# Butterflies on VectorE ahead of half-size TensorE steps, and S tiles split by DMA

## The chip, the cores and the metric

The kernel runs on one core of a Trainium2 chip. The metric is device time in microseconds. TensorE multiplies matrices from SBUF into PSUM, VectorE and ScalarE work on elements, GpSimd (POOL) is nearly unused before, SyncE (SP) issues DMAs in the order of its instructions. All DMAs run on 16 shared DMA engines. Every engine executes its own instructions strictly in program order.

## The reference

Two independent blocks, their results side by side in the last dimension:

```python
# A: Fourier mixing, real part; x is 2048 x 512
a = jnp.einsum("bsd,ed->bse", x, dft_hid_re)
b = jnp.einsum("bsd,ed->bse", x, dft_hid_im)
y = jnp.einsum("ts,bse->bte", dft_seq_re, a) - jnp.einsum("ts,bse->bte", dft_seq_im, b)
# B: a long convolution per channel (512 channels, length 2048, 128 states)
P = jnp.exp((A * dt[:, None])[:, :, None] * pos[None, None, :])
K = 2.0 * jnp.einsum("dn,dnl->dl", C, P).real
Kf = jnp.fft.rfft(K, L2)          # L2 = 4096
Uf = jnp.fft.rfft(u_t, L2)
y = jnp.fft.irfft(Uf * Kf[None, :, :], L2)[:, :, :L]
y = y + u * D_skip
```

Everything is float32. Inputs are random, but the DFT matrices of A are given as inputs.

## The kernel before

**Block A (class `Fnet`)** swaps the two products: it first multiplies S, the 2048 x 2048 sequence matrices (real and imaginary), with x, and then the result P with the small matrices W. Each product is made of three matmuls in the fast format `F32R`: an operand is split into `hi` (rounded to F32R) and `lo` (the rest), and hi·hi, hi·lo and lo·hi are summed in PSUM (L327, tile `acc`). x and W stay in SBUF; S and P stream by in tiles of 128 x 512. There are 8 groups of S (4 column blocks t, real and imaginary c) with 16 tiles each, 128 in all, and then 4 groups of P with 8 tiles each. A tile is used by 4 x 3 matmuls. Each finished group is copied out of PSUM by ScalarE (L350) and stored: S groups to the DRAM tiles `p` (L355), P groups to the output (L358).

A streamed tile goes through `load`: SP issues the DMA into `raw` (L295; 4 buffers, `RAWS`), ScalarE makes `hi` by a copy with rounding (L207), VectorE makes `lo = raw - hi` (L211). There are 3 pairs of hi and lo (`DEPTH`), given back when TensorE has used them. P tiles are read back from DRAM by the same path.

**Block B (class `Ssm`)** makes the kernel K from tables of powers of the state factors: VectorE builds tables by products and sums (`mul` L566, `add` L575) for 16 chunks of 32 channels, and TensorE sums over the states (`taps`, L762). Then it does the long convolution as an FFT in two steps, with fp32 matmuls on parts of the array (`tile_position`):

- first step on u, `stage1_u` (L835), 8 groups of two l2 pairs; result through ScalarE (L845) to DRAM `xu`;
- first step on K, `stage1_k` (L792), 8 groups of 64 channels; ScalarE (L801) into `xk_sb`, stored to DRAM `xk`. GpSimd adds the D skip to the first tap ahead of it (L785);
- second step on both, `product` (L913), for 4 quarters h of the channels and 4 parts q of the frequencies; ScalarE copies (L926), VectorE multiplies the two spectra (L929 to L942);
- first step of the inverse in the same function (L949), written through ScalarE (L964) to DRAM `zs`. While taps are left, its matmuls run right behind a `taps` group (`Joined`);
- last step of the inverse, `inverse` (L995), 2 groups per quarter h; ScalarE (L1001), output store (L1004).

The order of all this is made when the program is built: `Plan` simulates every engine with prices (`act`, `dve`, `load`, and numbers in the `yield` lines), and always emits next what it thinks can start first, with an urgency. What comes out is one fixed order for each engine and for SP's queue. A generator that yields a `Sem` waits there for a buffer; `banks` hands out two pairs of PSUM banks to all of block B, and `give` returns one. Block A's matmuls have a low urgency and fill TensorE whenever nothing of block B is ready.

## Time and profile before

| | |
|---|---|
| three runs | 594.92, 598.23, 600.19 us; median 598.23 |
| profiled execution, span from the first to the last instruction | 595.6 us |
| TensorE busy | 585.1 us (98%) |
| VectorE busy | 495.7 us (83%) |
| ScalarE busy | 381.0 us (64%) |
| GpSimd busy | 5.3 us (1%) |
| DMA | 125.97 MB, mean 212 GB/s |

The profile gives no time of the profiled execution other than its span; the launch and what lies after the last instruction are not in it. Busy times are sums over instructions, and matmuls overlap in the pipeline, so a busy TensorE is not yet one at its peak. A group of the table names line, engine, operation, what is written and read, the shape and the count; then its busy time, the mean duration in ns, and the idle time of the engine just before with what ended it. In the chain of work that ended last, every piece is a start, a duration, and an engine with its line.

### The profile page before, as it was taken

The numbers are of one execution on the slowest core, as the hardware profiler recorded it, in microseconds if no ns is written. First come the engines' busy times: TensorE is split into PE (matmuls) and PEld (weight loads), VectorE is DVE, ScalarE is ACT, GpSimd is POOL, SyncE is SP. The second block draws the span as 40 slices with busy tenths as digits, with TensorE's granted clock in tenths as the row PEclk, the third lists the DMA queues.
The fourth block names the chain that finished last, engine by engine and source line by source line (L and its number), as shares of the span: only waits on it lengthen the run. The fifth ranks groups of instructions, "written<-read, shape, count | busy, mean of one in ns | idle before, by whom it ended". The sixth has DMA issues, their size and how long they took to land.

```text
span 595.6 us, 16944 instructions
## 1 busy us (share of the span) xinstructions
PE 585.1 (98%) x6982; PEld 451.6 (76%) x6982; DVE 495.7 (83%) x883; ACT 381.0 (64%) x745; POOL 5.3 (1%) x12
## 2 busy tenths in 40 slices
PE   8999999999999999999899999999989999999997
PEld 6767668788788777777687787778767887777775
DVE  6977989999999999999699999999979973253620
ACT  5789884947586596758374976677655625354522
POOL 0000000000000000000000000000000000000000
PEclk9999999999999999999999999999989999999999
DMA  8999995363593376454778593478668745899674
GB/s 264 321 360 344 333 339 186 107 177 94 128 279 100 102 193 216 141 148 122 237 213 245 149 279 120 132 213 257 207 202 253 249 126 168 223 348 276 204 256 149
DMA packets 141246, 125.97 MB, mean 212 GB/s; under 512 B 46192, under 2 KB 106352, under 8 KB 140912
## 3 DMA queue, kind: packets, MB, share of 16 engines
q1 hardware_dynamic: 140880, 124.48, 68.2%
q8 instruction: 55, 0.90, 0.6%
q10 hardware_dynamic: 288, 0.39, 0.3%
q14 instruction: 23, 0.19, 0.1%
HBM read 82.12 MB, written 42.73 MB: 210 GB/s over the span
## 4 chain that ended last, share of the span: by engine, by line
PE 79%; DVE 12%; DMA 3%; issue 3%; ACT 2%; SPq 0%; DVEq 0%; ACTq 0%
PE acc L327 61%; PE f L913 4%; PE f L762 4%; DVE prod L566 4%; PE f L995 3%; DVE lo L211 3%; PE f L835 3%; DVE t L575 3%; PE f L949 2%; PE f L792 2%; DMA raw<-in_sT 1%; DMA xt_u<-xu 1%; DVE z L929 1%; DMA p<-y 1%; DMA xt_k<-xk 1%
## 5 line engine op out<-in xcount | busy, mean ns | idle before, releaser
L327 PE MATMUL acc<-hi,x_hi 128*128 128x512 f32 x640 | 257.7, 403 | 3.7 <-ACT y L350 1.9
L327 PE MATMUL acc<-lo,x_hi 128*128 128x512 f32 x640 | 250.7, 392 | 0.1
L327 PE MATMUL acc<-hi,x_lo 128*128 128x512 f32 x640 | 250.0, 391 | 0.1
L566 DVE TENSOR_TENSOR prod<-t,cs 128x1024 f32<-128x1024 f32 (+4 forms) x192 | 164.1, 871 | 7.5 <-ACT t L704 5.6
L327 PEld LDWEIGHTS acc<-hi,x_hi 128*128 128x128 f32 x640 | 120.2, 188 | 49.6 <-issue 20.1
L211 DVE TENSOR_TENSOR lo<-raw,hi 128x512 fp32r<-128x512 f32 x160 | 109.4, 687 | 53.8 <-ACT hi L207 48.9
L207 ACT ACTIVATE hi<-raw 128x512 fp32r<-128x512 f32 x160 | 100.3, 628 | 76.9 <-PE acc L327 56.8
L327 PEld LDWEIGHTS acc<-hi,x_lo 128*128 128x128 f32 x640 | 120.5, 188 | 26.7 <-issue 0.6
L327 PEld LDWEIGHTS acc<-lo,x_hi 128*128 128x128 f32 x640 | 120.5, 188 | 24.3 <-DVE lo L211 1.4
L575 DVE TENSOR_TENSOR t<-prod 128x512 f32<-128x512 f32 (+4 forms) x192 | 94.3, 513 | 1.2
L582 ACT ACTIVATE square<-t 128x256 f32<-128x256 f32 (+1 forms) x64 | 36.5, 571 | 25.3 <-DVE t L575 23.2
L350 ACT ACTIVATE y<-acc 128x512 f32<-128x512 f32 x47 | 27.7, 595 | 17.3 <-PE acc L327 9.8
L926 ACT ACTIVATE uk<-f 128x1024 f32<-128x1024 f32 x32 | 31.6, 1015 | 6.4 <-PE f L913 6.4
L762 PEld LDWEIGHTS f<-t,t 128*32 128x32 f32 x2048 | 29.4, 110 | 6.5 <-issue 5.0
L762 PE MATMUL f<-t,t 128*32 128x64 f32 x2048 | 32.2, 220 | 0.3 <-issue 0.3
L929 DVE TENSOR_TENSOR z<-uk 128x512 f32<-128x512 f32 x32 | 22.0, 687 | 12.4 <-ACT uk L926 10.1
L641 ACT ACTIVATE cs<-cs 128x352 f32<-128x352 f32 x32 | 15.9, 536 | 17.9 <-DVE cs L636 17.9
L964 ACT ACTIVATE z<-f 128x512 f32<-128x512 f32 x32 | 17.7, 594 | 11.4 <-PE f L762 7.4
L595 DVE TENSOR_TENSOR t<-square 128x128 f32<-128x128 f32 (+1 forms) x64 | 24.8, 387 | 0.0
L913 PE MATMUL f<-xt_k,w 64*32 64x128 f32 x1024 | 23.1, 271 | 0.5 <-issue 0.5
L589 DVE SCALAR_TENSOR_TENSOR t<-t 128x128 f32<-128x128 f32 (+2 forms) x48 | 22.4, 467 | 0.3
L931 DVE TENSOR_TENSOR uk<-uk 128x512 f32<-128x512 f32 x32 | 22.1, 689 | 0.7
(85 smaller groups left out, 444.8 us busy)
## 6 DMA issues: line engine op xcount, KB each, us to landing
raw<-in_sT SPq DMA_DIRECT2D x127, 256.0 KB, 3.7
p<-y SPq DMA_DIRECT2D x32, 256.0 KB, 4.1
xt_u<-xu SPq DMA_DIRECT2D x32, 256.0 KB, 4.4
xk<-xk_sb SPq DMA_DIRECT2D x32, 256.0 KB, 4.0
xt_k<-xk SPq DMA_DIRECT2D x32, 256.0 KB, 5.5
zs<-z SPq DMA_DIRECT2D x32, 256.0 KB, 3.4
zl<-zs SPq DMA_DIRECT2D x16, 512.0 KB, 6.1
raw<-p SPq DMA_DIRECT2D x32, 256.0 KB, 4.2
```

The costliest lines, as they stand in the source:

```text
L207: self.nc.scalar.activation(hi, src, AF.Copy)
L211: self.nc.vector.tensor_tensor(lo, src, hi.bitcast(F32), op=OP.subtract)
L327: nc.tensor.matmul(acc[d], l[:, cols], r, start=k == 0 and n == 0, stop=k == len(items) - 1 and n == 2)
L350: self.nc.scalar.activation(y, ps, AF.Copy, scale=-1.0 if g[2] == 1 else 1.0)
L566: self.nc.vector.tensor_tensor(p.rearrange("p k d c m -> p k (d c) m"), src.rearrange("p d c l -> p (d c) l")[:, None, :, rows].to_broadca ...
L575: self.nc.vector.tensor_tensor(dst[:, :, :, rows], p[:, 0], p[:, 1, :, ::-1], op=OP.add)
L582: self.nc.scalar.activation(sq, t[:, :, :, m // 2:m], AF.Square)
L595: self.nc.vector.tensor_tensor(t[:, :, 0, m:2 * m:2], box[0][:, :, 0], box[0][:, :, 1], op=OP.subtract)
L762: nc.tensor.matmul(ps[32 * j:32 * j + 32, i], t1[:, d, c], t2[:, d, c], start=c == 0, stop=c == 1, tile_position=(0, 32 * j))
L913: nc.tensor.matmul(got[r][1][32 * xx:32 * xx + 32, g, o:o + PART], self.w2[rows, 2 * q + r, xx, 32 * c:32 * c + 32], xt[rows, r, xx], star ...
L926: a.activation(uk[:, r].rearrange("p g n c d -> p g (n c d)"), p, AF.Copy)
L929: v.tensor_tensor(P[:, r], t[:, r], u[:, r], op=OP.mult)
```

## The change

Three things change together.

**Butterflies.** A Fourier step over 64 points is written as a step over 32 points on even and on odd inputs, and a sum and a difference of the two. The first steps on u and K are thereby half as large for TensorE: their matmuls contract 32 rows and have 64 columns instead of 128. ScalarE copies only the odd half from PSUM to SBUF, and VectorE makes the sum and then the difference, each from the even half in PSUM and the odd half in SBUF. For the last step of the inverse the butterfly sits ahead of it: parts q and q + 2 are combined. For q < 2 ScalarE copies the result of L949 into a kept tile `zk`; for q of 2 and 3 VectorE adds to `z` and subtracts in `zk`, and both are stored. The last step then contracts 64 rows and has 32 columns. The constants, the layouts in DRAM, the layout of `ks` and that of the output follow.

**S tiles by DMA.** The 112 S tiles after the first group no longer pass `raw`. GpSimd issues a DMA from DRAM that converts into `hi`; ScalarE writes `lo = -hi`; GpSimd issues a second DMA of the same source that adds into `lo`. The first S group, x, W and P keep the old path.

**Sizes.** `RAWS` 4 to 3, `DEPTH` 3 to 6, `AHEAD` 3 to 4, and 2048 bytes of DMA scratch.

```diff
@@ fft_constants
-    f = np.stack([np.cos(phi), -np.sin(phi)], axis=2).reshape(64, 128)
-    f1u = np.tile(f, (2, 1))
-    f1k = np.tile(f.reshape(32, 2, 128), (4, 1, 1))
+    f = np.stack([np.cos(phi), -np.sin(phi)], axis=2)[:, :32].reshape(32, 2, 64)
+    f1u = np.tile(f.transpose(1, 0, 2).reshape(64, 64), (2, 1))
+    f1k = np.tile(f, (4, 1, 1))
...
@@ Fnet.loads
+                if self.soft(i):
+                    yield self.ss
+                    self.plan.spawn(self.load_soft(src, i), urgency)
+                    continue
                 yield self.raws
                 self.plan.spawn(self.load(src, None, self.m, i, self.m_ev[i]), urgency)
+
+    def soft(self, i):
+        return i[0] == "s" and i[:3] != ("s", 0, 0) and True and i[:3] <= SOFT_TO
+
+    def load_soft(self, src, i):
+
+        hi, lo = (self.pool.tile([128, DM], F32R, name=m, bufs=DEPTH) for m in ("hi", "lo"))
+        yield "pool", ISSUE
+        self.nc.gpsimd.dma_start(hi, src)
+        yield "dma", load(256)
+        yield "act", act(512)
+        self.nc.scalar.activation(lo, hi.bitcast(F32), AF.Copy, scale=-1.0)
+        yield "pool", ISSUE
+        self.nc.gpsimd.dma_start(lo, src, accum_op=OP.add)
+        yield "dma", load(256)
+        self.m[i] = hi, lo
+        self.split_ahead += 1
+        self.plan.set(self.m_ev[i])
...
@@ Ssm.taps
-        nc.scalar.activation(ks[:, 8 * (n % 2):8 * (n % 2) + 8].rearrange("p (o i) l -> p o (i l)", o=2),
-                             p[:, :, 256:], AF.Copy)
+        nc.scalar.activation(ks[:, :, 8 * (n % 2):8 * (n % 2) + 8].rearrange("p l (o i) -> p l o i", o=2),
+                             p[:, :, 256:].rearrange("p o (i l) -> p l o i", i=4), AF.Copy)
@@ Ssm.stage1_k
-        yield "pe", 1.82, None, 32
+        yield "pe", 1.02, None, 64
         for a in range(2):
             for j in range(4):
-                r = slice(32 * j, 32 * j + 32)
-                nc.tensor.matmul(got[j // 2][1][:, j % 2], self.f1k[r, a], ks[r, :, 32 * a:32 * a + 32],
-                                 start=a == 0, stop=a == 1, tile_position=(32 * j, 0))
+                for y in range(2):
+                    r, o = slice(32 * j, 32 * j + 32), 32 * a + 16 * y
+                    nc.tensor.matmul(got[j // 2][1][64 * y:64 * y + 64, j % 2, 256 * a:256 * a + 256], self.f1k[r, a],
+                                     ks[r, o:o + 16].rearrange("p l i -> p (l i)"), start=True, stop=True,
+                                     tile_position=(32 * j, 64 * y))
...
-            for j in range(2):
-                yield "act", act(512)
-                o = 32 * h + 16 * j
-                nc.scalar.activation(xs[:, :, o:o + 16], p[:, j].rearrange("p (i l) -> p l i", i=16), AF.Copy)
+            even, odd = (p[:, :, 256 * a:256 * a + 256].rearrange("p j (l i) -> p j l i", l=16) for a in range(2))
+            lo, hi = (xs[:, a, :, 32 * h:32 * h + 32].rearrange("p l (j i) -> p j l i", j=2) for a in range(2))
+            yield "act", act(512)
+            nc.scalar.activation(hi, odd, AF.Copy)
+            yield "dve", dve(512)
+            nc.vector.tensor_tensor(lo, even, hi, op=OP.add)
+            yield "dve", dve(512), *APART
+            nc.vector.tensor_tensor(hi, even, hi, op=OP.subtract)
             self.give(k)
...
@@ Ssm.stage1_u
-        yield "pe", 1.82, None, 16
-        for m in range(2):
-            for r in range(2):
-                rows = slice(64 * r, 64 * r + 64)
-                nc.tensor.matmul(got[m][1][:, r], self.f1u[rows], u[rows, m], start=True, stop=True,
-                                 tile_position=(64 * r, 0))
+        yield "pe", 1.1, None, 32
+        for r in range(2):
+            for p in range(2):
+                for m in range(2):
+                    rows = slice(64 * r + 32 * p, 64 * r + 32 * p + 32)
+                    nc.tensor.matmul(got[r][1][64 * m:64 * m + 64, p], self.f1u[rows], u[rows, m], start=True, stop=True,
+                                     tile_position=(64 * r + 32 * p, 64 * m))
...
-            for r in range(2):
-                yield "act", act(512)
-                nc.scalar.activation(x[:, r], got[m][1][:, r], AF.Copy)
+            f = got[r][1]
+            yield "act", act(512)
+            nc.scalar.activation(x[:, 1], f[:, 1], AF.Copy)
+            yield "dve", dve(512)
+            nc.vector.tensor_tensor(x[:, 0], f[:, 0], x[:, 1], op=OP.add)
+            yield "dve", dve(512), *APART
+            nc.vector.tensor_tensor(x[:, 1], f[:, 0], x[:, 1], op=OP.subtract)
...
@@ Ssm.store_u
-        self.nc.sync.dma_start(self.xu.rearrange("s c l d -> (s c) l d")[:, 2 * m:2 * m + 2], x)
+        xu = self.xu.rearrange("(a s) c l d -> l (s c) a d", a=2)
+        for m in range(2):
+            self.nc.sync.dma_start(xu[l + 2 * m], x[64 * m:64 * m + 64])
...
@@ Ssm.product
         for n, (k, p) in enumerate(w.got):
-            yield "act", act(512)
-            a.activation(z[:, :, 2 * n:2 * n + 2].rearrange("p r x d -> p x r d"),
-                         p[:, :, :2 * PART].rearrange("p x (r d) -> p x r d", r=2), AF.Copy)
+            keep = zk[:, :, 2 * n:2 * n + 2].rearrange("p r x d -> p x r d")
+            new = p[:, :, :2 * PART].rearrange("p x (r d) -> p x r d", r=2)
+            if first:
+                yield "act", act(512)
+                a.activation(keep, new, AF.Copy)
+            else:
+                yield "dve", dve(512)
+                v.tensor_tensor(z[:, :, 2 * n:2 * n + 2].rearrange("p r x d -> p x r d"), new, keep, op=OP.add)
+                yield "dve", dve(512), *APART
+                v.tensor_tensor(keep, keep, new, op=OP.subtract)
             w.leave(k)
...
@@ Ssm.inverse
-        yield "pe", 0.1 + 0.1025 * n, None, 4 * n
-        for w in range(n // 2):
-            for y in range(2):
-                nc.tensor.matmul(ps[64 * y:64 * y + 64, w // 4, PART * (w % 4):PART * (w % 4) + PART],
-                                 self.ib[:, n * i + 2 * w + y], z[:, 2 * w + y], start=True, stop=True,
-                                 tile_position=(0, 64 * y))
+        yield "pe", 0.1 + 0.055 * n, None, 8 * n
+        for w in range(n // 4):
+            for x in range(4):
+                for y in range(2):
+                    r = slice(64 * y, 64 * y + 64)
+                    nc.tensor.matmul(ps[32 * x:32 * x + 32, y, PART * w:PART * w + PART],
+                                     self.ib[r, n * i + 4 * w + x], z[r, 4 * w + x], start=True, stop=True,
+                                     tile_position=(64 * y, 32 * x))
...
-RAWS, DEPTH, STAGED, AHEAD = 4, 3, 3, 3
+RAWS, DEPTH, STAGED, AHEAD = 3, 6, 3, 4
+ISSUE, SOFT_TO = 1.0, ("s", 3, 1)
...
-    nc = bacc.Bacc("TRN2", target_bir_lowering=False, num_devices=1)
+    nc = bacc.Bacc("TRN2", target_bir_lowering=False, num_devices=1, dynamic_dma_scratch_size=2048)
```

89 lines of the change are left out of this document (54 added, 35 removed).

## The prediction

> **What bounds the kernel now.** I read the engine summary first, then the table by stretches, then the chain of work that ended last in order of time.
>
> ```profile
> PE 585.1 (98%) x6982; PEld 451.6 (76%) x6982; DVE 495.7 (83%) x883; ACT 381.0 (64%) x745; POOL 5.3 (1%) x12
> q1 hardware_dynamic: 140880, 124.48, 68.2%
> ```
>
> ```profile
> 100.00:440.00 340.00, 335.80 (x4434) 263.94 (x4434) 331.08 (x591) 232.39 (x471) 4.82 (x7) 1.00 0.61 177
> 60.00:473.00 413.00, 408.67 (x5264) 317.53 (x5264) 398.99 (x704) 281.60 (x567) 4.82 (x7) 1.00 0.65 193
> 490.00:596.00 106.00, 101.07 (x1377) 78.01 (x1365) 35.44 (x54) 46.03 (x74) 0.24 (x1) 0.99 0.75 230
> ```
>
> The columns after the stretch's length are busy time of TensorE, its weight loads, VectorE, ScalarE and GpSimd, then the granted clock, the DMA engines' share and GB/s. TensorE has work everywhere. But from 100 to 440 us VectorE is busy 331 of 340 us as well: two engines are full there, and whoever relieves only one of them gains little. After 490 us VectorE is a third busy and TensorE stands alone. GpSimd is idle throughout, and the clock is whole.
>
> The chain shows how long each group of matmuls holds TensorE when nothing is late (start, duration, engine and line, instructions; one fp32 matmul call stands as two instructions):
>
> ```profile
> 27.97 1.92 PE f L835 x8
> ...
> 50.13 1.92 PE f L835 x8
> ...
> 60.43 1.92 PE f L835 x8
> ...
> 289.56 1.05 PE f L949 x32
> ...
> 296.10 1.96 PE f L913 x128
> ...
> 307.17 1.90 PE f L995 x32
> ...
> 329.92 1.90 PE f L995 x32
> ...
> 334.08 1.93 PE f L792 x16
> ...
> 350.26 20.67 PE acc L327 x90
> ...
> 417.50 1.90 PE f L995 x32
> ...
> 438.25 3.06 PE f L995 x32
> ...
> 489.80 1.92 PE f L762 x128
> ...
> 503.04 1.93 PE f L792 x16
> ...
> 541.47 2.27 PE acc L327 x9
> ```
>
> An acc matmul costs 20.67/90 = 0.23 us, so one S tile (12 of them) holds TensorE 2.76 us; the short stretch of 9 shows 0.2 us more for each change between kinds. The last taps (L762) end at 491.7 us: VectorE's tables are finished only then, and what remains is TensorE's. The 16 tiles of the first S group, 192 acc matmuls, are through shortly before the u group at 60.43 us, and 384 for P with the small groups among them count back from the end to about 473 us: between lies the S stretch that the change touches.
>
> **The change, part by part.** *First step on u (L835, 8 groups).* Half the contraction and half the output columns leave 8 calls of 32 rows by 64 columns, 512 wide, in place of 4 of 64 by 128. The trace has that tile at L949, 16 calls 256 wide, the same column count in all:
>
> ```profile
> L949 PE MATMUL f<-uk,ia 32*64 32x256 f32 x512 | 17.9, 387 | 0.0
> L913 PE MATMUL f<-xt_k,w 64*32 64x128 f32 x1024 | 23.1, 271 | 0.5 <-issue 0.5
> L995 PE MATMUL f<-zl,ib 128*64 128x128 f32 x256 | 17.3, 288 | 0.2 <-issue 0.2
> ```
>
> So 1.05 for 1.92 us; 0.96 if it halves exactly, 1.92 if the small tiles did not run side by side, which L949 excludes. I take 1.05: 8 x 0.87 = 7.0 us. *First step on K (L792, 8 groups).* Here the new form is L949's own, 32*64 by 256: 8 x (1.93 - 1.05) = 7.0 us. *Last step of the inverse (L995, 8 groups).* 32 calls in the 64*32, 128-wide form of L913, which needs 1.96 us for 64: 0.98, or up to 1.1 with a fixed part. 8 x (1.90 - 0.98) = 7.4 us. TensorE sheds **21.4 us** of a path on which it is 98% busy. The number of changes between acc and small matmuls stays.
>
> *VectorE.*
>
> ```profile
> L211 DVE TENSOR_TENSOR lo<-raw,hi 128x512 fp32r<-128x512 f32 x160 | 109.4, 687 | 53.8 <-ACT hi L207 48.9 <-DMA xt_k<-xk 4.1 <-DMA raw<-in_sT 0.4
> L964 ACT ACTIVATE z<-f 128x512 f32<-128x512 f32 x32 | 17.7, 594 | 11.4 <-PE f L762 7.4 <-PE f L949 4.0
> L575 DVE TENSOR_TENSOR t<-prod 128x256 f32<-128x256 f32 x32 | 13.5, 421 | 0.0
> L346 DVE COPY y<-acc 128x256 f32<-128x256 f32 x1 | 0.4, 424 | 11.5 <-ACT y L343 11.5
> 226.72 1.20 DVE lo L211 x2
> DVE z L929 <- ACT uk L926: 10.1, 5, 4.4
> ```
>
> 112 of the 128 S tiles lose their lo subtraction. Added are 4 butterflies of 512 columns for each of 8 u groups, 8 K groups and the 8 products with q of 2 or 3: 96. None of before's VectorE rows of this width reads PSUM; the one PSUM read, 256 wide, takes 424 ns, as one of 256 from SBUF does (421), so I price them like L211. Back to back two take 1.20 us, 0.60 each. Whole kernel: (96 - 112) x 0.60 = -9.6 us. Before the last taps, where VectorE binds: all 112 go, and about 86 come (32 for u, 30 for K, 24 for the products of the first three quarters): -26 x 0.60 = **-15.6 us**. TensorE's own saving up to there is 7.0 + 7 x 0.88 + 4 x 0.92 = 16.9 us, by the chain's dates (all of u, seven K groups, the four inverse groups listed). The two full engines shrink together; the slower one sets the pace, at a cost of 1.3 us. From 20 to 100 us the u butterflies add 32 x 0.60 = 19 us to a VectorE that has little room, and only a dozen lo's (7 us) leave: the tables slip some 4 us there and win it back later; the room after 100 us covers it. Each butterfly waits in VectorE's order for ScalarE's copy of the odd half, and table products queue behind it. The like wait is the last row, 10.1 us for 32 halves, or 7.6 us for 24 groups; the waits of L211 that go, 48.9 us for 160 tiles, are worth 34 us for 112. I count neither. The PSUM pair of a group is held for a copy and two butterflies, 2.0 us, against two copies, 1.2 us; acc work fills the 0.8 us.
>
> *ScalarE* loses one evacuation of two in each of those 24 groups, 48 x 0.59 = 28 us; for S it writes -hi into lo instead of hi, 0.63 us as now. It is 64% busy, so I count nothing. *SP's queue* loses 112 loads and gains 24 smaller issues:
>
> ```profile
> L295 SPq DMA_DIRECT2D raw<-in_sT x127: 327/334/1141, 2.1 to 452.9; - x127
> L207 ACT ACTIVATE hi<-raw x160: 613/632/665, 3.8 to 579.5; 128x512 fp32r<-128x512 f32 x160
> DMA to landing us min/median/max: 2.5/3.8/7.7
> SPq L295 <- DVE lo L211: 158.7, 77, 5.8
> ```
>
> The last row is SP standing on a raw buffer 158.7 us in all with every other store queued behind it; that mostly goes. I count nothing for it, since TensorE hardly waits for a store. Three raw buffers instead of four serve only the first group, the weights and P: 3.8 + 0.63 + 0.69 us over three is 1.7 us per tile, under 2.76.
>
> *GpSimd's queue and the DMA engines* carry what is new. Each of 112 tiles takes two issues, two landings and a ScalarE pass between them, in order on a queue where the second issue waits for ScalarE and the next tile's first issue (and L785's additions) stand behind it. Before shows no GpSimd DMA, no cast and no accumulation. Issue: nearest row below is SP's 0.33 us, nearest far row above SP's longest L295 issue, 2.14 us:
>
> ```profile
> L295 SPq DMA_DIRECT2D raw<-p x32: 319/382/2135, 457.6 to 568.7; - x32
> ```
>
> S is consumed over 413 us, 3.69 us a tile, so two issues are covered up to 1.8 us each; I cost them at nothing. Chain: at SP's issue and the median landing 2 x (0.33 + 3.8) + 0.63 = 8.9 us. Six hi/lo pairs give five other tiles' 13.8 us of cover, so issue plus landing may reach 6.6 us before TensorE stalls. Transfer: a plain stretch gives the price of one load.
>
> ```profile
> 100.00:120.00 20.00, 19.82 (x213) 14.96 (x212) 19.83 (x38) 16.64 (x37) 0.74 (x1) 1.00 0.32 104
> DMA packets 1126, 2.07 MB, mean 104 GB/s; under 512 B 128, under 2 KB 128, under 8 KB 1124
> ```
>
> 0.32 x 20 us for 2.07 MB is 0.81 us of all 16 engines per 256 KB. One extra transfer per tile is 112 x 0.81 = 91 us; the S stretch has 0.35 x 413 = 145 us idle. From below the accumulation costs one copy (91 us), from above two (it reads its target too, 181 us) or more. I take the copy, nearest to the only row there is; the other end is a rival.
>
> The sum: 595.6 (span) - 21.4 + 1.3 = 575.5 us. The median of the runs shown, 598.23, lies 2.6 us over this span; **forecast 578 us**, 3.4% faster. TensorE's idle time could come back on top: 1920 x 0.23 = 442 us, the small groups 16 x (1.92 + 1.96 + 1.05) + 8 x (1.92 + 1.93 + 1.90) = 125 us, some 60 changes of kind 12 us and about 8 us of start and end leave 9 us of the span. So the low end is 568.
>
> **The rivals.** *1, slower: DMA engines become the bound.* For it: they are at 0.65 in the S stretch, and 0.93 in the first 60 us.
>
> ```profile
> 0.00:60.00 60.00, 58.38 (x238) 42.50 (x239) 47.45 (x105) 46.56 (x95) 0.20 (x4) 1.00 0.93 323
> ```
>
> With the accumulation at two copies 181 us go into 145: the stretch lengthens by 36 us, and TensorE waits for lo tiles. What it sheds outside the stretch (four u groups 3.5, the last K group 0.9, four inverse groups 3.7) still counts: 595.6 + 36 - 8 = 624, 626 on the runs' scale. It decides from an accumulation of about 1.5 copies. Against it: nothing in the row says that an add must cost a second pass. The Trainium skill, "Collectives: The Full Stack", section "The bandwidth ceiling", says that a DMA add is slow because it needs two source reads, not because of the adding; by that the sum would be this rival's, and no run here shows it yet.
>
> *2, no change: the longer chain stalls TensorE.* With the longest landing seen, 7.7 us, the chain is 16.7 us; a tile pair comes free every (16.7 + 2.76)/6 = 3.24 us against 2.76 in dense stretches. That is 0 to 112 x 0.48 = 54 us, by half the tiles in dense stretches and half of those late 14 us: 575.5 + 14 = 590, or 592. For it: busy stretches raise a landing of the same size.
>
> ```profile
> xt_k<-xk SPq DMA_DIRECT2D x32, 256.0 KB, 5.5
> ```
>
> At that median the chain is 12.3 us, still covered. Against: the mean interval of 3.69 us absorbs it.
>
> *3, far slower: GpSimd's issuing is the bound.* At 2.14 us an issue, 224 take 479 us, 66 more than the stretch: 654, or 656. It decides above 1.8 us. The Trainium skill, "SBUF — State Buffer", section "Who interferes with whom", has a rule against this change: descriptors issued from GpSimd cannot be written while VectorE holds their shared port pair in a two-port mode. It lists scalar forms for that, not two-input ones, and leaves the sum alone unless the kind that fills 331 of 340 us here blocks too; no run here shows it yet.
>
> *4, the steps do not halve*, small tiles taking turns: nothing gained, 597. L949 and L913 speak against it.
>
> **How the numbers follow.** Forecast 0.62, with its own range 568 to 588; rival 1 0.20, rival 2 0.10, rival 3 0.06, rival 4 0.02. About 1% is what a measurement of this kernel can tell from no change. Faster by over 1%: the forecast and a third of rival 2, 0.66. Within 1%: the rest of rival 2 and rival 4, 0.09. Slower: rivals 1 and 3, 0.25. The range for 8 in 10 runs from 568 to 628: it holds the forecast, rival 2 and the doubled accumulation, and leaves out rival 3, a dearer accumulation and a little below.
>
> **What the next profile would show.** Right: L835's, L792's and L995's successors at about 1.05, 1.05 and 1.0 us a group in the chain; VectorE some 10 us less busy in all, with two-input rows of 512 from PSUM at 0.69 us; DMA share in the S stretch at about 0.87; taps ending near 475 us; no wait of TensorE's weight loads on hi or lo. Rival 1 shows a share of 0.95 or more from 60 to 470 us and TensorE waiting on DMA lo; rival 2 short such waits in dense stretches alone; rival 3 GpSimd's queue never idle, with the DMA engines free. The prediction is wrong if TensorE's sum falls by 21 us and its idle time grows by as much.

## The result, and the profile after

The changed kernel takes **640.86 us** (median of four runs, 632.99 to 644.77), the kernel before 599.21 us (594.92 to 600.56) beside it. The ratio is 1.0685, with a 95% interval from 1.063 to 1.0741: 6.9% slower, where 3.4% faster was forecast. One of the four runs, 644.77 us, counts as slow (its granted clock was 0.959), and the ratio leaves it out. The profiled execution took 640.51 us with a span of 638.6 us, 43.0 us more than before's span.

The engine summary and the queues of the kernel after:

```profile
PE 584.6 (92%) x7430; PEld 448.3 (70%) x7430; DVE 493.1 (77%) x867; ACT 357.2 (56%) x697; POOL 163.2 (26%) x236
...
q1 hardware_dynamic: 127184, 94.56, 49.9%
q0 software_dynamic: 32256, 58.73, 43.8%
...
PE 30%; issue 23%; DVE 17%; DMA 12%; POOL 12%; ACT 4%; SPq 1%; POOLq 0%; DVEq 0%; ACTq 0%
```

Two things stand here. First, the DMA engines. Before, the one queue held them for 68.2% of 595.6, or 406 us; now the two queues hold them for 93.7% of 638.6 (49.9 and 43.8), or **598 us**. That is more than the whole span of the kernel before. These shares add up the time of all packets, each put where it starts, so in a short stretch they can read above 1. Second, TensorE's busy time hardly fell (585.1 to 584.6 us), although its matmuls did get cheaper, as the chain of waits shows (start, duration, engine, line, instructions):

```profile
344.45 1.05 PE f L819 x32
...
365.72 1.05 PE f L990 x32
...
514.09 1.09 PE f L1057 x64
```

L819 is the first step on K (1.93 before), L1057 the last step of the inverse (1.90 before), L990 the unchanged step beside them. What they saved was used up by a slower clock: the acc matmuls, 1920 as before, were busy for 460.9 us then and for 473.8 us now. The table by stretches (busy time of TensorE, its loads, VectorE, ScalarE, GpSimd; then granted clock, DMA share, GB/s):

```profile
0.00:60.00 60.00, 56.89 (x277) 41.73 (x277) 54.54 (x115) 41.04 (x81) 7.72 (x15) 1.00 0.98 315
60.00:100.00 40.00, 37.09 (x300) 26.32 (x293) 31.71 (x56) 25.98 (x55) 13.72 (x19) 0.91 1.08 298
100.00:500.00 400.00, 360.63 (x4967) 280.67 (x4966) 343.78 (x603) 237.09 (x480) 141.03 (x202) 0.96 0.98 229
500.00:639.00 139.00, 129.99 (x1897) 99.61 (x1896) 63.09 (x96) 53.04 (x84) 0.76 (x2) 1.00 0.78 233
```

From 60 to 500 us the DMA engines are at 0.98 or more, where before had 0.65 from 60 to 473 us. They are full of time and not of bytes: 229 GB/s here at 0.98, against 323 GB/s at 0.93 in the first 60 us of the kernel before. VectorE is no longer full (343.78 of 400 us). TensorE is idle for 39.4 of the 400 us, and its mean granted clock over the whole span is 0.967 against 0.996 before; 0.029 x 638.6 is 19 us, nearly as much as the small matmuls shed. The last taps (L788) begin at 511.6 us instead of 491.5, the last acc matmul at 634.3 instead of 591.4.

The waits (engine and line, what it waited for, us in total, times, longest) say who stands in that stretch:

```profile
POOL hi L300 <- PE acc L351: 145.0, 67, 12.8
POOL lo L305 <- ACT lo L303: 127.8, 61, 9.9
...
ACT lo L303 <- DMA hi<-in_sT: 25.4, 17, 3.9
...
PE acc L351 <- ACT y L374: 13.1, 6, 4.5
PEld acc L351 <- DMA lo<-in_sT: 13.0, 12, 3.2
```

GpSimd waits at both of its issues: for TensorE to give back a pair, and for ScalarE's -hi, which itself waits for a landing. TensorE's weight loads wait for lo's landing, but the longest wait of its matmuls is for ScalarE to copy a finished S group (y). The issues and the landings:

```profile
L305 POOL DMA_DIRECT2D lo<-in_sT x112 | 98.6, 899 | 155.5 <-ACT lo L303 127.8 <-ACT square L608 7.0 <-ACT t L730 4.2
L300 POOL DMA_DIRECT2D hi<-in_sT x112 | 68.9, 624 | 177.6 <-PE acc L351 145.0 <-DVE lo L213 29.1 <-issue 2.0
```

```profile
hi<-in_sT POOLq DMA_DIRECT2D x112, 256.0 KB, 5.8
lo<-in_sT POOLq DMA_DIRECT2D x112, 256.0 KB, 6.0
```

An issue takes 0.62 and 0.90 us, well under rival 3's 1.8. Issue plus landing is 6.4 and 6.9 us, at the edge of the 6.6 that six pairs were said to cover.

### The profile page after: what moved, and what is told of

It reads as the page before. It is cut to its first block, busy times and chain, and to the rows that moved or that the text cites. A ratio compares the mean times of both kernels' runs of the same rounds, so it can differ in the third digit from the quotient of the medians.

```text
span 638.6 us, 17973 instructions
## 1 busy us (share of the span) xinstructions
PE 584.6 (92%) x7430; PEld 448.3 (70%) x7430; DVE 493.1 (77%) x867; ACT 357.2 (56%) x697; POOL 163.2 (26%) x236
## 3 DMA queue, kind: packets, MB, share of 16 engines
q1 hardware_dynamic: 127184, 94.56, 49.9%
q0 software_dynamic: 32256, 58.73, 43.8%
## 4 chain that ended last, share of the span: by engine, by line
PE 30%; issue 23%; DVE 17%; DMA 12%; POOL 12%; ACT 4%; SPq 1%; POOLq 0%; DVEq 0%; ACTq 0%
PE acc L351 22%; POOL lo L305 6%; DVE prod L592 5%; POOL hi L300 5%; PE f L954 3%; DVE t L601 3%; DMA zl<-zs 3%; DMA hi<-in_sT 3%; DMA p<-y 2%; PE f L990 2%; DMA par<-par_dram 2%; PE f L788 2%; PE f L1057 1%; DMA lo<-in_sT 1%; DVE lo L213 1%
## 5 line engine op out<-in xcount | busy, mean ns | idle before, releaser
L351 PE MATMUL acc<-hi,x_hi 128*128 128x512 f32 x640 | 261.7, 409 | 17.1 <-ACT y L374 13.1
L351 PE MATMUL acc<-lo,x_hi 128*128 128x512 f32 x640 | 255.0, 398 | 8.5 <-DMA lo<-in_sT 8.3
L351 PE MATMUL acc<-hi,x_lo 128*128 128x512 f32 x640 | 254.4, 397 | 3.0 <-issue 3.0
L351 PEld LDWEIGHTS acc<-hi,x_hi 128*128 128x128 f32 x640 | 122.5, 191 | 59.5 <-ACT y L374 16.4
L351 PEld LDWEIGHTS acc<-lo,x_hi 128*128 128x128 f32 x640 | 122.6, 192 | 39.9 <-DMA lo<-in_sT 12.4
L305 POOL DMA_DIRECT2D lo<-in_sT x112 | 98.6, 899 | 155.5 <-ACT lo L303 127.8
L300 POOL DMA_DIRECT2D hi<-in_sT x112 | 68.9, 624 | 177.6 <-PE acc L351 145.0
L303 ACT ACTIVATE lo<-hi 128x512 fp32r<-128x512 f32 x112 | 69.4, 624 | 33.9 <-DMA hi<-in_sT 25.4
L213 DVE TENSOR_TENSOR lo<-raw,hi 128x512 fp32r<-128x512 f32 x48 | 32.9, 689 | 37.6 <-ACT hi L209 37.5
L209 ACT ACTIVATE hi<-raw 128x512 fp32r<-128x512 f32 x48 | 30.2, 630 | 39.7 <-PE acc L351 30.4
L788 PEld LDWEIGHTS f<-t,t 128*32 128x32 f32 x2048 | 30.8, 113 | 10.3 <-issue 4.8
L788 PE MATMUL f<-t,t 128*32 128x64 f32 x2048 | 33.7, 225 | 3.2 <-DVE t L601 3.2
L970 DVE TENSOR_TENSOR z<-uk 128x512 f32<-128x512 f32 x32 | 22.0, 688 | 10.5 <-ACT uk L967 9.7
L954 PEld LDWEIGHTS f<-xt_k,w 64*32 64x32 f32 x1024 | 17.8, 108 | 10.0 <-DMA xt_k<-xk 7.3
```

Source lines behind the costliest of these rows:

```text
L209: self.nc.scalar.activation(hi, src, AF.Copy)
L213: self.nc.vector.tensor_tensor(lo, src, hi.bitcast(F32), op=OP.subtract)
L300: self.nc.gpsimd.dma_start(hi, src)
L303: self.nc.scalar.activation(lo, hi.bitcast(F32), AF.Copy, scale=-1.0)
L305: self.nc.gpsimd.dma_start(lo, src, accum_op=OP.add)
L351: nc.tensor.matmul(acc[d], l[:, cols], r, start=k == 0 and n == 0, stop=k == len(items) - 1 and n == 2)
```

## The experiments

Medians are in us; every ratio is to runs of the kernel before on the same chip (595.4 to 596.1 us), with its 95% interval. The whole change was timed on another chip, where the kernel before took 599.21 us; differences to it are therefore taken from the ratios.

### The two halves of the change

Butterflies alone, with plain loads, VectorE's lo, and the sizes of before:

```diff
-        return i[0] == "s" and i[:3] != ("s", 0, 0) and True and i[:3] <= SOFT_TO
+        return i[0] == "s" and i[:3] != ("s", 0, 0) and True and False and i[:3] <= SOFT_TO
...
-RAWS, DEPTH, STAGED, AHEAD = 3, 6, 3, 4
+RAWS, DEPTH, STAGED, AHEAD = 4, 3, 3, 3
```

> All three butterflies, every S tile on the old path with the old sizes. Theory A (the DMA engines are the bound of the changed kernel, because the added S transfers cost 2.5 us of all 16 engines per tile against 0.81 us of the plain load they replace): the DMA share from 100 to 440 us falls back to about 0.6, TensorE sheds its 21 us, VectorE rises to about 560 us busy and is now the bound up to the last taps; 585 to 610 us. Theory D (the butterflies themselves are what is slow: stores of xk and xu wait up to 18 us for VectorE in SP's order and everything behind them waits too): 635 us or more, like the whole change.

Measured: 636.1, ratio 1.0677 [1.0612, 1.0742]. The split alone, the kernel before with the new `loads`, `load_soft`, sizes and scratch:

```diff
+                if self.soft(i):
+                    yield self.ss
+                    self.plan.spawn(self.load_soft(src, i), urgency)
+                    continue
...
-RAWS, DEPTH, STAGED, AHEAD = 4, 3, 3, 3
+RAWS, DEPTH, STAGED, AHEAD = 3, 6, 3, 4
```

> The kernel before with the 112 S tiles split by DMA and the new sizes, no butterflies. Theory A: the DMA share is about 1 from 60 to 500 us as in the whole change, although VectorE is relieved by 67 us and TensorE's work is that of before; 630 to 650 us. Theory D: with VectorE relieved and no butterfly in the way, 575 to 598 us.

Measured: 648.15, ratio 1.083 [1.0751, 1.0908]. The stretch from 100 to 500 us, of the butterflies alone and then of the split alone:

```profile
100.00:500.00 400.00, 389.50 (x5087) 310.38 (x5086) 393.00 (x697) 251.90 (x498) 3.72 (x7) 1.00 0.62 178
```

```profile
100.00:500.00 400.00, 365.37 (x5184) 281.43 (x5182) 318.70 (x562) 249.92 (x503) 137.31 (x197) 0.97 1.00 231
```

Each half loses by itself, and by a different engine. The butterflies fill VectorE (393 of 400 us; 553.3 us in all, 57.6 more than before), with the DMA engines at 0.62: the last taps begin at 536.7 us. The time is the one that theory D named, but its cause is small in the trace: SP waits 11.4 us here for VectorE ahead of K stores, and 53.3 us in the whole change, where this row stands:

```profile
SPq L839 <- DVE xk_sb L831: 53.3, 6, 18.1
```

The loss is as large with 11.4 us of such waits as with 53.3; VectorE, full up to the last taps, explains this kernel better. The split relieves VectorE (433.4 us in all) and fills the DMA engines to 1.00. Together they cost about as much as either alone. Our reading is that the split takes back what the butterflies put on VectorE and puts its own load on the DMA engines.

### What a split tile's two transfers cost

In the first kernel the second transfer is left out, so lo stays -hi. In the second, it is there but overwrites lo without adding.

```diff
-        yield "pool", ISSUE
-        self.nc.gpsimd.dma_start(lo, src, accum_op=OP.add)
-        yield "dma", load(256)
```

> The whole change without the second transfer: lo stays -hi (wrong numbers, the same matmuls). Theory A: 112 converting transfers stand in the software queue with about 0.81 us of all engines each, 91 us; total traffic as before, share about 0.65 in the S stretch; 572 to 585 us, which shows what the butterflies and the relieved VectorE are worth without the extra traffic. Theory C: 140 us in the software queue, time in the same range. Theory D: 600 us or more, since the butterflies stay.

```diff
-        self.nc.gpsimd.dma_start(lo, src, accum_op=OP.add)
+        self.nc.gpsimd.dma_start(lo, src)
```

> The whole change, but the second transfer of each tile overwrites lo with a converted copy of the source instead of adding to it (so lo holds the wrong numbers; the same instructions, bytes of source and waits otherwise). Theory A with the accumulation as the dear transfer (it reads its target as well, two copies): the software queue falls from 280 us of all engines to about 182 us, the share in the S stretch to about 0.85, the time to 575 to 595 us. Theory C (converting is what is dear, 1.25 us for each transfer): the queue stays at 280 us and the time at 630 to 645 us. Theory B (not the engines' time but the chain of two landings and the in-order waits): the queue falls, the time stays above 610 us.

Measured: 594.14 without it, ratio 0.9967 [0.994, 0.9994]; 610.68 with it but without the add, ratio 1.0237 [1.02, 1.0274]. GpSimd's queue in the first and in the second:

```profile
q0 software_dynamic: 16128, 29.37, 19.5%
```

```profile
q0 software_dynamic: 32256, 58.73, 36.0%
```

The price of a transfer follows by queue share times span over count. One that converts: 0.195 x 592.3 / 112 = **1.03 us** per 256 KB; two that convert: 0.360 x 609.7 / 224 = 0.98 us. The whole change: 0.438 x 638.6 = 280 us, less 112 x 1.0, leaves **1.5 us** for one that adds. A plain load was 0.81. So a tile costs 2.5 us of the 16 engines in place of 0.81, and 112 tiles add 189 us where 91 were forecast and 145 idle. That price is not made by full engines: where fewer tiles are split and the share in the same stretch is 0.76 to 0.84 (three kernels below), a tile costs 2.6 to 2.7 us by the same sum. The steps in time are, by the ratios, some 16 us for the second transfer and some 27 more for its add.

The first kernel came out above the 572 to 585 us of theory A. For the second, A's 575 to 595 and C's 630 to 645 both missed, and B's mark, above 610, was just met. So it could still be latency, since the add ends a longer chain. Therefore, in the next kernel, lo stays -hi again and the same adding transfer goes to spare tiles that no tile waits for (`DEPTH` 5, to have room for them):

```diff
-        yield "pool", ISSUE
-        self.nc.gpsimd.dma_start(lo, src, accum_op=OP.add)
-        yield "dma", load(256)
...
+        yield self.scs
+        sc = self.sc.pop(0)
+        yield "pool", ISSUE
+        self.nc.gpsimd.dma_start(sc, src, accum_op=OP.add)
...
```

> The whole change with the accumulating transfer aimed at one of two spare tiles that nothing reads; lo stays -hi (wrong numbers, the same matmuls), and a tile is ready for TensorE after its first landing and ScalarE's pass. Five hi/lo pairs in place of six. Theory A (the engines' time is the bound, and the add costs 1.5 us of it wherever it lands): DMA share about 1 in the S stretch, 625 to 645 us. Theory B (the chain of two landings and the in-order waits are the bound, the traffic is covered): about as without the second transfer, 590 to 602 us.

Measured: 633.09, ratio 1.0584 [1.0526, 1.0643], with this row in the same stretch:

```profile
100.00:500.00 400.00, 364.82 (x4792) 287.03 (x4791) 347.38 (x615) 237.06 (x483) 146.09 (x206) 0.96 1.00 228
```

With no tile waiting for the add, some 37 of the 43 us stay, and the DMA engines are full. It is their time, and not the length of one tile's chain, that carries most of the loss. The smaller `DEPTH` is not behind it: without the second transfer five pairs took 594.14 us as well (below). One reserve: GpSimd's queue is still held by the two spare tiles' own adds, as its waits show, so a part of the 37 us may be that queue. TensorE's matmuls themselves wait only 0.6 us there for the ScalarE pass of an S tile.

```profile
POOL sc L314 <- DMA sc<-in_sT: 69.7, 42, 4.6
```

### Doses, the planner's prices and the sizes

Every third tile split, the rest by VectorE. These are 5 of the 16 tiles in each of 7 groups, 35 in all and not the 37 of the expectation:

```diff
+        return i[0] == "s" and i[:3] != ("s", 0, 0) and True and i[3] % 3 == 1 and i[:3] <= SOFT_TO
```

> The whole change with only every third S tile split by DMA (37 tiles in place of 112). The looks so far put a converting transfer at 1.0 us and an accumulating one at 1.5 us of all 16 DMA engines, so 37 tiles add 62 us to the engines' time, which fits into the 145 us that are idle; but VectorE keeps two thirds of its subtractions beside the 58 us of butterflies. Theory A (three resources are each nearly full: TensorE, VectorE up to the last taps, DMA; the change moves work from the first to the second and from the second to the third): VectorE about 528 us busy, full to about 520 us, 605 to 620 us. If only the DMA engines were the trouble: 575 to 590 us.

Measured: 631.83, ratio 1.059 [1.0534, 1.0646], 12 us above the range of theory A. The DMA engines are at 0.76 from 100 to 500 us now, but VectorE is back at 534.9 us and the last taps at 533.6: it is the butterflies' case again. Fewer split tiles trade one full engine for the other.

The planner priced each of the two transfers as a plain load. With dearer prices in its place:

```diff
-        yield "dma", load(256)
+        yield "dma", load(340)
...
-        yield "dma", load(256)
+        yield "dma", load(490)
```

> The whole change, with the planner's prices for the two transfers set to what was measured (1.03 and 1.5 us of the DMA engines instead of 0.78 and 0.78), so that the order of all queues is made for them. Theory A (the engines' time is the bound): the same traffic, share about 1 from 60 to 500 us, within 15 us of the whole change, 625 to 650 us. Rival F (the order was made for wrong prices and the stalls come from that): 600 to 615 us.

Measured: 692.42, ratio 1.1522 [1.1394, 1.165], outside both ranges. A planner that prices the transfers dearer makes a worse order, so nothing here says that cheap prices in the plan are what costs the time; why this order is so much worse was not followed up.

Four staging tiles for finished S groups in place of three, since TensorE waits for ScalarE's copy (y) at group ends. First with the second transfer left out and `DEPTH` 5, then the kernel before (with the smaller DMA scratch, which makes the room), then the whole change with `DEPTH` 5:

```diff
-RAWS, DEPTH, STAGED, AHEAD = 3, 6, 3, 4
+RAWS, DEPTH, STAGED, AHEAD = 3, 5, 4, 4
```

> The kernel without the second transfer (lo stays -hi, as in e4_no_second, 594 us), with four staging buffers for finished groups in place of three, and five hi/lo pairs in place of six. Theory G (what still stands between 594 us and 574 us is TensorE waiting at the ends of S groups: the fourth accumulator's copy waits until a store of P has landed, 6.6 us at 166 us, 3.2 us at 57 us, and the granted clock drops after each such pause): 582 to 588 us, with TensorE's waits on the copies of finished groups down from 15 us to under 4 us. Rival E (other late transfers take their place): 590 us or more.

```diff
-RAWS, DEPTH, STAGED, AHEAD = 4, 3, 3, 3
+RAWS, DEPTH, STAGED, AHEAD = 4, 3, 4, 3
```

> The kernel before with four staging buffers for finished groups in place of three, and the smaller DMA scratch that makes room for the fourth. Theory G: before stalls little at the ends of groups (4.7 us in all), so 590 to 596 us, at best 1% faster than before; a loss would show that a changed order alone moves this kernel by several us.

```diff
-RAWS, DEPTH, STAGED, AHEAD = 3, 6, 3, 4
+RAWS, DEPTH, STAGED, AHEAD = 3, 5, 4, 4
```

> The whole change with four staging buffers in place of three and five hi/lo pairs in place of six. Theory A: the DMA engines stay the bound, 628 to 645 us. Theory B or G: the stalls at group ends carry the loss, under 620 us.

Measured: 594.14 (0.995 [0.9922, 0.9978]), 601.65 (1.0082 [1.0056, 1.0109]) and 673.88 (1.1275 [1.1222, 1.1328]). In the first the waits for y are gone (0.3 us in place of 14.6) and nothing is gained: TensorE now waits 11.2 us at the end for the inverse's tiles (`PE f L1054 <- DMA zl<-zs`). So theory G, that these waits stand between 594 and 574 us, failed. The second says what a new order alone does to a kernel: 5 us here. The third missed both of its ranges; the y wait is gone there too, and TensorE's wait for lo has grown from 8.3 us in the whole change:

```profile
PE acc L351 <- DMA lo<-in_sT: 39.9, 20, 8.1
```

With the DMA engines full, one pair of hi and lo fewer and one staging tile more cost some 35 us. By this row the length of the chain does count there, as rival 2 had it; how much of the 35 us is the new order was not separated.

### VectorE relieved without the DMA engines

Both kernels load plainly and have all butterflies. In the first, with the sizes of after, lo is left out on the 112 tiles and hi is multiplied in its place; in the second, with the sizes of before, GpSimd computes lo.

```diff
...
+        if where is self.m and self.soft(key):
+            yield "act", act(512)
+            self.nc.scalar.activation(to[0], raw, AF.Copy)
+            to = [to[0], to[0]]
+        else:
+            yield from self.split(*to, raw)
```

> The butterflies, and for the 112 S tiles the old plain load by SP with ScalarE's hi, but no lo at all: TensorE reads hi in its place (wrong numbers, the same matmuls). VectorE is relieved as in the whole change, the DMA engines carry what they did before, and GpSimd issues nothing. Theory A: TensorE's 21 us come through, 572 to 582 us, and the kernel without the second transfer (594 us) loses its gain to the converting path: 1.0 us instead of 0.81 per load, two more steps in order on GpSimd. Rival E (what eats the gain has nothing to do with how S is fetched: late stores of P and late loads of the spectra stall TensorE in the shortened schedule): 588 to 598 us again.

```diff
+        if pool:
+            yield "pool", 1.2
+            self.nc.gpsimd.tensor_tensor(lo, src, hi.bitcast(F32), op=OP.subtract)
...
```

> The butterflies with the old loads and sizes; the subtraction lo = raw - hi of the 112 S tiles runs on GpSimd instead of VectorE, with no transfer added. No run has shown such an instruction of 512 columns on GpSimd. If it runs beside VectorE undisturbed: VectorE about 485 us busy, DMA share 0.62, 575 to 590 us, which would beat both kernels. If GpSimd and VectorE hold each other up while both read SBUF: VectorE's two-input instructions grow beyond 0.69 us and the time is 620 us or more.

Measured: 600.62 (1.0069 [1.0033, 1.0105]) and 682.48 (1.1441 [1.139, 1.1491]). The second fails for a reason of its own; two groups of it (busy time, mean ns):

```profile
L592 DVE TENSOR_TENSOR prod<-t,cs 128x1024 f32<-128x1024 f32 x96 | 135.0, 1408 | 1.0
...
L214 POOL TENSOR_TENSOR lo<-raw,hi 128x512 fp32r<-128x512 f32 x112 | 180.4, 1618 | 337.2 <-ACT hi L209 332.6 <-DMA p<-y 4.5
```

and the first of them in the kernel before:

```profile
L566 DVE TENSOR_TENSOR prod<-t,cs 128x1024 f32<-128x1024 f32 x96 | 117.1, 1221 | 1.1
```

A subtraction takes 1618 ns on GpSimd beside a busy VectorE, against 687 on VectorE, and VectorE's own products go from 1221 to 1408 ns while it runs beside them; VectorE's busy time is 589.0 us although it has 112 operations fewer than with the butterflies alone, where it was 553.3. The Trainium skill, "SBUF — State Buffer", section "Who interferes with whom", says that a VectorE instruction with two inputs in SBUF contends with a GpSimd instruction that reads SBUF; these rows agree.

The first is the one that matters for the forecast: neither extra traffic nor the 112 subtractions, TensorE's steps halved, and still no faster than before. By the sum such a kernel would take 574 to 578 us; theory A's 572 to 582 failed, and 600.62 lies 3 us above the range of its rival E.

### Which engine must be relieved

Three kernels with the loads and the sizes of before make a square with it. In the first, ScalarE copies stand in place of the butterflies (TensorE relieved alone); in the second, lo is left out besides (both relieved); the third is the kernel before without lo (VectorE relieved alone).

```diff
-            yield "dve", dve(512)
-            nc.vector.tensor_tensor(lo, even, hi, op=OP.add)
-            yield "dve", dve(512), *APART
-            nc.vector.tensor_tensor(hi, even, hi, op=OP.subtract)
+            yield "act", act(512)
+            nc.scalar.activation(lo, even, AF.Copy)
...
```

> TensorE's steps on u and K and the inverse's last stay at half size, but ScalarE copies stand in place of VectorE's butterflies (the sums and differences are left out), and the S tiles are loaded and split as before, with the sizes of before: TensorE sheds 21 us, VectorE keeps its load of before. Theory H (the path through VectorE's tables to the last taps, with some 100 us behind them, sets the end as much as TensorE): 588 to 596 us, last taps begin near 490 us, TensorE idle before them. Rival (TensorE alone is the bound): 572 to 578 us. Rival (only the order's luck): 590 to 602, with no pattern over this run and the next two.

The second has this edit and the lo edit above:

> The run before, and VectorE's subtraction for lo is left out on the 112 S tiles too (hi is multiplied twice): TensorE sheds 21 us, VectorE 67 to 77 us. Theory H: 560 to 578 us, for both paths shrink together, last taps 25 us or more earlier than before's. Rival (TensorE alone): 572 to 578 us, the same as the run before it. Rival (the order's luck): 590 to 602.

The third has the lo edit alone:

> The kernel before, with VectorE's subtraction for lo left out on the 112 S tiles (hi is multiplied twice): VectorE sheds 67 to 77 us, TensorE nothing. Theory H: 588 to 596 us, for TensorE is nearly full by itself. Rival (TensorE alone): 593 to 597 us. Rival (the order's luck): 590 to 602. A time under 585 would say that VectorE alone was the bound.

The fourth has all butterflies, no lo, and the sizes of before:

```diff
-RAWS, DEPTH, STAGED, AHEAD = 3, 6, 3, 4
+RAWS, DEPTH, STAGED, AHEAD = 4, 3, 3, 3
```

> All butterflies on VectorE and the half-size steps, plain loads, VectorE's subtraction for lo left out on the 112 S tiles (hi is multiplied twice), and the sizes of before (4, 3, 3, 3). It differs from the run that took 577 us (half steps, no lo, no butterflies) only in the butterflies, which put 58 us back on VectorE, and from the one at 601 us only in the sizes. Theory H (VectorE's load, about 490 us here, is the second bound): 592 to 602 us. Rival (the sizes, or the fewer raw buffers, cost the 24 us): 575 to 582 us.

| kernel | TensorE busy | VectorE busy | time | ratio |
|---|---|---|---|---|
| before | 585.1 | 495.7 | 595.4 | |
| VectorE relieved alone | 580.2 | 431.9 | 596.08 | 1.0013 [0.9993, 1.0033] |
| TensorE relieved alone | 570.7 | 496.0 | 607.21 | 1.0187 [1.0147, 1.0227] |
| both relieved | 562.8 | 432.8 | 577.38 | 0.9704 [0.9662, 0.9746] |
| half steps, butterflies for lo, sizes of before | 566.1 | 490.0 | 585.85 | 0.9838 [0.9744, 0.9931] |
| the same, sizes of after (above) | 570.7 | 490.8 | 600.62 | 1.0069 [1.0033, 1.0105] |

Only with both engines relieved does TensorE's saving come through nearly whole (18.0 of 21.4 us); VectorE alone gives nothing, TensorE alone costs 12 us. Against the forecasts: TensorE relieved alone missed all three of its ranges, upwards; VectorE relieved alone lies in that of TensorE as the only bound; both relieved lies in that of the two bounds (theory H) and in that of TensorE as the only bound, and the last but one row, 586, missed H's 592 to 602 as well as its rival's 575 to 582. The chain of what ended last, as shares by engine, shows which path was tight. Of the kernel before:

```profile
PE 79%; DVE 12%; DMA 3%; issue 3%; ACT 2%; SPq 0%; DVEq 0%; ACTq 0%
```

Of the kernel with VectorE relieved alone:

```profile
PE 81%; DVE 13%; ACT 2%; issue 2%; DMA 1%; SPq 0%; DVEq 0%; ACTq 0%
```

Of the kernel with TensorE relieved alone:

```profile
PE 39%; DVE 31%; ACT 10%; DMA 8%; issue 8%; SPq 3%; ACTq 0%; DVEq 0%
```

Of the kernel with both relieved:

```profile
PE 82%; DVE 8%; ACT 5%; DMA 2%; issue 1%; POOL 0%; ACTq 0%; POOLq 0%
```

Take TensorE's 21 us away alone, and VectorE's part of the chain goes from 12% to 31%; the last taps begin at 505.2 us (491.5 before) and behind them lie 101 us in which the inverse waits for its tiles and the clock falls. With both relieved they begin at 445.2 us and TensorE stays dense to the end, at a clock of 1.000. These two rows of TensorE's last 46 us are of the kernel with TensorE relieved alone:

```profile
560.00:580.00 20.00, 17.00 (x472) 11.91 (x454) 9.67 (x16) 11.30 (x16) 0.00 (x0) 1.00 0.62 188
580.00:606.00 26.00, 7.22 (x188) 3.87 (x188) 2.66 (x4) 4.34 (x8) 0.00 (x0) 0.55 0.67 203
```

So two bounds meet here, by the square and by its chains. That VectorE is the second of them rests above all on one corner, TensorE relieved alone, with its loss, its late taps and VectorE's 31% of the chain. Each corner of the square is one planned order, though, and a new order alone moved the kernel before by 5 us, so a part of the 12 and the 18 us may be order. And it isn't the whole of it. The butterflies for lo's leave VectorE where it was, and such kernels came out at 586, 594, 601 and, with lo kept and no butterflies, 607. The last two rows of the table differ in the sizes alone and by 14.8 us. With little room on either engine, what is left over seems to hang on the order that the planner happens to make, or on the buffers themselves (three raw tiles or four), by up to some 20 us; which of them, and which feature of an order, was not settled.

### A smaller share of the change

By the measured prices a mix could fit: only the inverse's butterfly (TensorE sheds 7 us, VectorE takes 22), and as many split tiles as the idle DMA time holds. Every second tile, then every third, with the sizes of after:

```diff
...
+        return i[0] == "s" and i[:3] != ("s", 0, 0) and i[3] % 2 == 1 and i[:3] <= SOFT_TO
```

> Only the inverse has its butterfly (8 of the 24 halved groups: TensorE sheds 7 us, VectorE takes 32 operations or 22 us), and every second S tile past the first group is split by DMA (56 tiles: VectorE sheds 38 us, the DMA engines take 56 x 1.7 = 95 us more), sizes of after. Both full engines shrink, by 7 and 16 us, and the S stretch's 145 us of idle DMA time holds the extra transfers. Theory H with the measured transfer prices: 586 to 592 us. Rival (the changed order and the longer chain of a split tile cost more than that): 596 to 610 us.

```diff
...
+        return i[0] == "s" and i[:3] != ("s", 0, 0) and i[3] % 3 == 1 and i[:3] <= SOFT_TO
```

> The same with every third S tile (37 tiles: VectorE sheds 25 us and takes 22, the DMA engines take 63 us more). Theory H: 592 to 598 us, for VectorE is hardly relieved. Rival (the split tiles' number sets the cost): between the run before it and 597 us.

Measured: 601.59 (1.0087 [1.0062, 1.0112]) and 599.55 (1.0049 [1.0021, 1.0076]). Both missed what theory H gave them, 586 to 592 and 592 to 598, and lie where their rivals had them: the split tiles and the changed order cost more than their relief brought. Of the first, TensorE's busy time is 579.1 us, 6 less than before, and VectorE's 484.1, 11.6 less, so both were relieved and the DMA engines were at 0.78 to 0.86 through the S stretch; yet TensorE stood idle 19 us instead of 10.5. No kernel with the whole computation beat the kernel before in these runs.

## Why the prediction was wrong, by its steps

**The steps on u, K and the inverse: right.** 1.04, 1.05 and 1.09 us a group (the first from the kernel without the second transfer) against 1.05, 1.05 and 0.98 to 1.1. With both engines relieved TensorE is busy 562.8 us against 580.2 without the half steps, 17.4 less, and against before's 585.1, 22.3 less; 21.4 was the sum.

**VectorE: right, a little dear.** The butterflies' rows from PSUM are 0.69 us, as priced:

```profile
L833 DVE TENSOR_TENSOR xk_sb<-f,xk_sb 128x512 f32<-128x512 f32 x16 | 11.1, 692 | 0.6
...
L1018 DVE TENSOR_TENSOR z<-f,zk 128x512 f32<-128x512 f32 x16 | 11.0, 687 | 9.7 <-PE f L990 9.1 <-ACT ks L798 0.6
```

96 of them added 57.6 us (0.60 each, as forecast), 112 lo's took 63.8 us away (0.57 each, not 0.60): -6.2 in place of -9.6. Where the DMA engines had room the last taps began at 469.9 us, near the forecast 475.

**GpSimd's issues: right at nothing; rival 3 fell.** 0.62 and 0.90 us, far under 1.8. The section of the Trainium skill that rival 3 names, "SBUF — State Buffer", "Who interferes with whom", lists copies and casts beside the scalar form; with VectorE mostly on two-input work no issue here came near the price of that rival.

**The transfers: wrong, and the first cause.** The step that failed is the term "One extra transfer per tile is 112 x 0.81 = 91 us", set against 145 us of idle time. The conversion was not priced at all (1.0 in place of 0.81 us, on both transfers), and the accumulation was taken at the copy's end of its bounds (0.81 us) and costs 1.5, conversion included. 189 us do not go into 145. Rival 1 had the place and its two-copies price (181 us) nearly right: 626 forecast, 641 measured. It said that it decides from an accumulation of about 1.5 copies; 1.5 us is 1.85 copies, and 1.5 of the conversion's. The share of 0.95 or more, its sign, is there (0.98 to 1.08). Its other sign, TensorE waiting for lo, is there but small, 8.3 us of the 54 that TensorE stands idle; 13.1 us are the wait for ScalarE's copies of finished S groups. What it left out is the clock: 0.96 over 400 us is 16 us of TensorE's rate, about its 15 us of miss (worked out, not tried by itself). The rule that the prediction drew from the Trainium skill, "Collectives: The Full Stack", section "The bandwidth ceiling", spoke for this rival. That section explains a ring step of a collective; for the transfer here the trace bears it out in direction, since an add costs more than a copy that overwrites, by 0.5 us and not by a whole second copy.

**The two engines that "shrink together": wrong, and the second cause.** By the ratios (forecast 0.966, without the second transfer 0.997, measured 1.0685), some 43 of 61 us between forecast and result come with the second transfer. The other 18 stand in the kernel that leaves it out. The sentence that failed is "the two full engines shrink together; the slower one sets the pace, at a cost of 1.3 us". The view that it was worked out from was right (331 of 340 us on VectorE), and so was its own warning that who relieves one of two full engines gains little. But the change relieves VectorE by 3 to 6 us net, and in the square TensorE's 21 us pay out at 18 where VectorE sheds 63. Three kernels with the change's relief of both engines and no add (586, 594 and 601 us) lie 12 to 26 us above 595.6 - 21.4, by their ratios, where the step said 1.3. Whether VectorE's load, the order or the buffers set that cost stays open. Which wait takes it in place of TensorE's work was not settled either: the kernels at 594 to 601 us lose it at the ends of S groups, or at the inverse's tiles in the end, and a cure of the one brought the other.

**SP's queue: counted at nothing, and it was not.** In the whole change SP stands 53.3 us for the butterflies ahead of K stores (the row among the experiments), a wait that the prediction did not count. And "gains 24 smaller issues" overlooked that the K store is written in another layout. Its issues before and after (min/median/max ns):

```profile
L806 SPq DMA_DIRECT2D xk<-xk_sb x32: 371/624/1687, 120.3 to 509.5; - x32
```

```profile
L839 SPq DMA_DIRECT2D xk<-xk_sb x32: 580/1228/5812, 133.6 to 530.8; - x32
```

In the kernel without the second transfer one sees what that does. SP's timeline (start, duration, queue, line), and TensorE in the table by stretches over the same time:

```profile
161.24 4.49 SPq L836 DMA_DIRECT2D xk<-xk_sb  x4
165.83 3.93 SPq L376 DMA_DIRECT2D p<-y  x3
```

```profile
160.00:180.00 20.00, 13.42 (x109) 10.48 (x109) 17.60 (x29) 11.54 (x21) 2.29 (x4) 0.83 0.69 184
```

Four K stores hold SP for 4.49 us ahead of the store of a finished S group; TensorE waits 6.6 us for that group's buffer, and its clock is 0.83 in these 20 us. With both engines relieved the same layout costs nothing that can be seen, so this is one way of losing time in a tight order, not by itself the cause of the 18 us.

**Rivals 2 and 4.** Where the DMA engines have room and six pairs stand, no wait of TensorE on hi or lo shows among its largest; with them full its matmuls wait 8.3 us for lo with six pairs and 39.9 us with five. So rival 2 shows only on top of rival 1. Rival 4 fell with the first step.

## What to carry to other kernels

Price a transfer that converts or adds by a measurement of its own before handing an engine's work to the DMA engines, and sum their share times the span: here 406 + 189 us of DMA time left nothing idle of 596. Where the profile shows two engines full over the same stretch, a change that relieves one and merely swaps work on the other should be priced from nothing upwards, not at the whole saving: such kernels came out between 586 and 601 us against 595. A kernel whose order is planned when it is built moved by 1 to 8% here when a price or a buffer count changed, so compare a change with kernels that change the order alone.

## What the runs showed of the hardware

- A DMA of 256 KB that converts float32 to the fast format held the 16 engines for 0.98 to 1.03 us, one that also adds into SBUF for 1.5 to 1.7 (a split tile's 2.5 to 2.7 less 1.0), a plain one for 0.81.
- After a pause of several us TensorE's granted clock was lower for a while: 0.83 in the 20 us with a 6.6 us pause, 0.55 in the last 26 us of the kernel with TensorE relieved alone, where it works 7.2 us in all. There 64 instructions of the inverse's last step take 1.09 us at 555 us, and 32 take 1.19 us soon after a pause of 12.4 us, so that pause was paid for a second time:

```profile
555.41 1.09 PE f L1047 x64
...
600.26 1.19 PE f L1047 x32
```

- Beside a busy VectorE a two-input operation of 512 columns on GpSimd took 1618 ns, against 687 on VectorE, and VectorE's own two-input operations of 1024 columns went up by 15% (1221 to 1408 ns).
